# Moving the residual rows and the normalisation between queues and engines in a convolution, Fourier-transform and MLP kernel

## The chip, the core and the metric

The kernel runs on one core of one Trainium2 chip. A core has a matrix engine (TensorE, "PE" in the profile, with "PEld" for the loading of its weights), VectorE ("DVE"), ScalarE ("ACT"), GpSimd ("POOL") and SyncE ("SP"), which computes nothing here and only issues transfers. Each engine works through its own list of instructions in order. Transfers are issued from the lists of SP, ACT and POOL ("SPq", "ACTq", "POOLq" in the profile are the queues of these engines). The metric is the device time in microseconds; the time before is the median of three runs.

## The reference

The input `x` is (8, 4224, 192): eight batches of 4224 rows of 192. Step one is a causal convolution over seven rows with one softmax-weighted filter for each of eight groups of columns. Step two takes its result as the new `x`:

```
X = fft(fft(x, axis=1), axis=2)
u = x + real(X)
un = (u - mean(u)) / sqrt(var(u) + 1e-6)      # over the 192 columns
out = u + relu(un @ w_ch1) @ w_ch2            # 192 -> 768 -> 192
```

All of it is computed for all eight batches in float32, and the big products are made from float16 pairs (a high part and a rest).

## The kernel before

Batches follow each other. For one batch the front part works on whole columns: the convolution as matmuls with a banded matrix (`pc`), whose result `xa` is stored to a scratch tensor `sc` in device memory; loads of `sc` in transform order (`xs`, line 456); their split into a high part `XH` on ScalarE (line 472) and a rest `XL` on VectorE (line 473), both scaled; a first transform stage (`pa`, line 490, copied out as `yh`, `yl`) and a second one (`pb`, line 516, copied out as `V`).

Then come nine tiles for each batch (`it` 0 to 8), the first eight with four groups of 128 rows and the last with one. For a tile, `prep` makes the third transform stage (`pq`, line 574), moves it scaled into `u` (ScalarE, line 591), adds the residual rows `xr` (GpSimd, line 592), takes mean and variance (VectorE, lines 598 and 599), makes the factor `y` and the offset `nm` (lines 610 to 618: the square root on ScalarE, the reciprocal on VectorE, the rest on GpSimd), normalises (`un`, line 628, on ScalarE, apart from the first two tiles of all), and splits into float16 parts `hl` (line 638 on ScalarE, line 641 on GpSimd). A transposing transfer on SP makes `kt` from `hl`. The residual rows are rows of `sc` in an order that four index lists give; `load_res` (line 544) gathers them with one indirect transfer for each group, issued from GpSimd.

The MLP of a tile is `mlp_hidden` (`ph`, line 680; `hh` on ScalarE, line 684; `hlo` on VectorE, line 685) and `mlp_out` (`po`, lines 699, 702 and 705; the sum `u<-po,fo,u` on VectorE, line 711; the store of `u` on SP). `ph` has two buffers in the matrix engine's output memory, and the tag `f` (`pc`, `pa`, `pb`, `pq`) four.

The loop at line 882 gives the order in which all this is written: in step n the MLP's hidden part of tile n, the output part of tile n-1, the normalisation of tile n+2, the transform and sums of tile n+3 and the residual rows of tile n+4 are interleaved with the front part of a later batch. A scheduler then orders every engine's list anew.

Of the kernel before, what the change touches and what calls it, by code (L numbers as in the profile page):

```python
# [125 lines left out]
def kernel(  # L126
# [314 lines left out]
    def load_x(bt, i):  # L441
# [5 lines left out]
        for ch in range(NA // AC):  # L447
# [7 lines left out]
            with tc.issue_after(turn[0]) if b == 1 else ExitStack():  # L455
                load = (nc.scalar if b else nc.sync).dma_start(xs[AC * ch : AC * (ch + 1), : b1 - b0], src)
# [81 lines left out]
    def load_res(bt, it, g):  # L538

        b = bt.b  # L540
        if g == 0:
            bt.xr[it] = sb.tile([128, 4, D], F32, tag="xr", name=f"xr_{b}_{it}", bufs=3)
        col = 0 if it == Q0 else 1 + 4 * it + g
        nc.gpsimd.indirect_dma_start(  # L544
            bt.xr[it][:, g], None, bt.sc[:S],
            bass.IndirectOffsetOnAxis(ap=rows_sb[:, col : col + 1], axis=0),
        )

    def prep(bt, it):
        b = bt.b  # L550
        xr = bt.xr.pop(it)
# [2 lines left out]
        u = sb.tile([128, 4, D], F32, tag="u", name=f"u_{b}_{it}", bufs=5)
# [35 lines left out]
        for to, src in moves:  # L590
            nc.scalar.activation(to, src, AF.Copy, scale=bt.g)  # L591
        nc.gpsimd.tensor_tensor(u[:, :ng], u[:, :ng], xr[:, :ng], op=ALU.add)  # L592
        bt.u[it] = u
# [10 lines left out]
        sd = sb.tile([128, 4], F32, tag="sd", name=f"sd_{b}_{it}", bufs=3)[:, :ng]  # L604
        y = sb.tile([128, 4], F32, tag="y", name=f"y_{b}_{it}", bufs=3)[:, :ng]
        t = sb.tile([128, 4], F32, tag="t", name=f"t_{b}_{it}", bufs=3)[:, :ng]
        w = sb.tile([128, 4], F32, tag="w", name=f"w_{b}_{it}", bufs=3)[:, :ng]
        nm = sb.tile([128, 4], F32, tag="nm", name=f"nm_{b}_{it}", bufs=3)[:, :ng]
        G_ = nc.gpsimd
# [367 lines left out]
```

## Time and profile before

| what | value |
|---|---|
| median of three runs | 1347.4 us (1347.21 to 1353.27) |
| span of the profiled execution | 1331.2 us |
| PE busy | 1198.8 us (90%) |
| ACT busy | 813.4 us (61%) |
| DVE busy | 742.1 us (56%) |
| POOL busy | 660.3 us (50%) |
| mean granted clock of PE | 0.965 |

The span runs from the first to the last instruction of the program on the core. The median lies 16.2 us above it; that is the time around the program. The batches repeat: from about 330 us to 1104 us the same pattern returns every 157 us. Busy time of PE contains modelled ends of pipelined matmuls. A row of a waits view reads "engine line waited for: us in total, times, longest"; a row of a timeline reads "start, length, engine, line, operation, out<-in, count [idle before <- what ended it]"; a row of the groups ends with "busy us, mean ns of one | idle before".

### The profile page before, as it was taken

What the parts mean: (1) busy time and instruction counts of PE and PEld (TensorE: products, weight loads), DVE (VectorE), ACT (ScalarE), POOL (GpSimd) and SP (SyncE); (2) the same over time, 40 slices, a digit from 0 to 9 for tenths busy, and PEclk for the clock granted to TensorE, in tenths of its full rate; (3) what the DMA queues carried; (4) which work ended last, traced back from release to release, by engine and by line L of the source; (5) the groups of instructions that cost most, each with busy time, mean ns of one, the idle gap of its engine ahead of it and who ended that gap; (6) DMA issues with size and microseconds to landing.
All of it is one profiled execution on the core that took longest, in us unless ns stands there. A gap on an engine that the chain in (4) does not pass through costs nothing.

```text
span 1331.2 us, 30081 instructions
## 1 busy us (share of the span) xinstructions
PE 1198.8 (90%) x12224; PEld 942.5 (71%) x12224; DVE 742.1 (56%) x1635; ACT 813.4 (61%) x1562; POOL 660.3 (50%) x1052
## 2 busy tenths in 40 slices
PE   4177889998999989998999989999789998999999
PEld 4175667786878767775877868777577876778667
DVE  7765555466545755456643674446654576555444
ACT  4645766567656775558765676656764667545642
POOL 0255534556345744456435563456634576456520
PEclk9598999998999989999999989999999999999999
DMA  8946855556655555465563566454674443223321
GB/s 270 247 128 152 207 121 122 128 118 158 143 125 118 157 129 135 99 147 147 123 142 103 125 165 142 119 122 114 157 138 109 117 108 84 71 65 81 75 63 40
DMA packets 225819, 170.19 MB, mean 128 GB/s; under 512 B 119560, under 2 KB 207440, under 8 KB 225680
## 3 DMA queue, kind: packets, MB, share of 16 engines
q1 hardware_dynamic: 132048, 85.82, 27.1%
q10 hardware_dynamic: 80960, 56.48, 17.7%
q0 software_dynamic: 12672, 25.97, 7.2%
q8 instruction: 95, 1.56, 0.5%
q14 instruction: 44, 0.36, 0.1%
HBM read 83.73 MB, written 58.55 MB: 107 GB/s over the span
## 4 chain that ended last, share of the span: by engine, by line
POOL 28%; PE 26%; issue 18%; ACT 12%; DMA 8%; DVE 5%; ACTq 1%; POOLq 0%; SPq 0%; DVEq 0%
POOL xr L544 12%; PE ph L680 10%; POOL u L592 6%; DMA sc<-xa 5%; ACT un L628 4%; POOL hl L641 4%; PE po L699 3%; PE po L702 3%; PE po L705 3%; PE pq L574 2%; PE pb L516 2%; ACT hh L684 2%; ACT XH L472 2%; ACT hl L638 2%; DMA xs<-sc 1%
## 5 line engine op out<-in xcount | busy, mean ns | idle before, releaser
L680 PE MATMUL ph<-kt,W 128*128 128x512 f16 (+1 forms) x2160 | 502.3, 366 | 20.3 <-DVE hlo L685 12.4
L685 DVE SCALAR_TENSOR_TENSOR hlo<-ph,hh 128x512 f16<-128x512 f32 (+1 forms) x400 | 271.0, 679 | 405.1 <-ACT hh L684 403.9
L699 PE MATMUL po<-W,hh 128*128 128x192 f16 x1584 | 389.3, 249 | 47.1 <-ACT hh L684 44.3
L702 PE MATMUL po<-W,hh 128*128 128x192 f16 x1584 | 388.8, 249 | 0.0
L705 PE MATMUL po<-W,hlo 128*128 128x192 f16 x1584 | 384.7, 248 | 0.2 <-DVE hlo L685 0.2
L684 ACT ACTIVATE hh<-ph 128x512 f16<-128x512 f32 (+1 forms) x400 | 234.8, 590 | 216.0 <-PE ph L680 147.5
L544 POOL DMA_INDIRECT xr<-sc,rows_sb x264 | 270.5, 1025 | 134.0 <-issue 59.5
L680 PEld LDWEIGHTS <-W 128*128 128x128 f16 x2160 | 195.7, 98 | 169.5 <-issue 32.4
L641 POOL TENSOR_TENSOR hl<-un,hl 128x512 f16<-128x512 f32 (+1 forms) x144 | 126.8, 902 | 187.7 <-ACT hl L638 187.5
L699 PEld LDWEIGHTS <-hh 128*128 128x128 f16 x1584 | 157.1, 99 | 68.0 <-ACT hh L684 49.8
L592 POOL TENSOR_TENSOR u<-u,xr 128x768 f32<-128x768 f32 (+1 forms) x72 | 124.2, 1726 | 154.1 <-ACT u L591 154.0
L628 ACT ACTIVATE un<-u,nm,y 128x192 f32<-128x192 f32 x256 | 120.2, 537 | 98.9 <-POOL nm L618 94.7
L705 PEld LDWEIGHTS <-hlo 128*128 128x128 f16 x1584 | 156.1, 99 | 26.4 <-issue 3.1
L702 PEld LDWEIGHTS <-hh 128*128 128x128 f16 x1584 | 156.7, 99 | 17.6 <-issue 3.3
L387 PE MATMUL pc<-xt,band 128*120 128x144 f32 x756 | 116.4, 292 | 21.4 <-DMA band<-line_d 15.2
L490 PE MATMUL pa<-c_sb,XH 128*128 128x128 f16 x1024 | 104.9, 223 | 24.5 <-ACT XH L472 20.6
L387 PEld LDWEIGHTS pc<-xt,band 128*120 128x120 f32 x756 | 103.0, 186 | 29.0 <-issue 15.2
L473 DVE SCALAR_TENSOR_TENSOR XL<-xs,s_x,XH 128x768 f16<-128x768 f32 x64 | 101.4, 1603 | 20.7 <-ACT XH L472 15.5
L472 ACT ACTIVATE XH<-xs,s_x 128x768 f16<-128x768 f32 x64 | 104.9, 1682 | 9.7 <-DMA xs<-sc 9.7
L490 PEld LDWEIGHTS <-XH 128*128 128x128 f16 x1024 | 83.1, 99 | 36.4 <-ACT XH L472 21.1
L711 DVE SCALAR_TENSOR_TENSOR u<-po,fo,u 128x384 f32<-128x384 f32 (+1 forms) x136 | 81.3, 599 | 40.9 <-PE po L705 39.0
L499 DVE SCALAR_TENSOR_TENSOR yl<-pa,yh 99x512 f16<-99x512 f32 x128 | 85.5, 682 | 30.8 <-ACT yh L498 30.4
(125 smaller groups left out, 1467.2 us busy)
## 6 DMA issues: line engine op xcount, KB each, us to landing
out_dram<-u SPq DMA_DIRECT2D x64, 384.0 KB, 2.4
xt<-in_xw_dram SPq DMA_DIRECT2D x42, 576.0 KB, 7.8
sc<-xa ACTq DMA_DIRECT2D x42, 540.0 KB, 6.1
xs<-sc ACTq DMA_DIRECT2D x84, 192.0 KB, 3.9
xs<-sc ACTq DMA_DIRECT2D x28, 216.0 KB, 3.7
xr<-sc,rows_sb POOLq DMA_INDIRECT x264
sc<-xa ACTq DMA_DIRECT2D x7, 450.0 KB
xt<-in_xv_dram SPq DMA_DIRECT2D x6, 504.0 KB, 4.2
```

The lines of the kernel that those rows point to most:

```text
L387: nc.tensor.matmul(pc[:WR, h - h0], band[:, h, :WR], xt[:, :, h * GRP : (h + 1) * GRP], start=True, stop=True,)
L490: nc.tensor.matmul(pa[:, i], x[:, at], F[:, l], start=(n == 0), stop=(n == 2))
L544: nc.gpsimd.indirect_dma_start(bt.xr[it][:, g], None, bt.sc[:S], bass.IndirectOffsetOnAxis(ap=rows_sb[:, col : col + 1], axis=0),)
L592: nc.gpsimd.tensor_tensor(u[:, :ng], u[:, :ng], xr[:, :ng], op=ALU.add)
L628: nc.scalar.activation(un[:, g], u[:, g], AF.Identity, bias=nm[:, g : g + 1], scale=y[:, g : g + 1],)
L641: nc.gpsimd.tensor_tensor(bl[:, :, o : o + n], un[:, :ng, f], hi[:, :, f], op=ALU.subtract)
L680: nc.tensor.matmul(ph[:, n], W1[:, w, ht * 128 : (ht + 1) * 128], kt[:, k], start=(i == 0), stop=(i == len(order) - 1),)
L684: anchor[0] = nc.scalar.activation(hh, ph, AF.Relu).ins
L685: nc.vector.scalar_tensor_tensor(hlo, ph, 0.0, hh, op0=ALU.max, op1=ALU.subtract)
L699: nc.tensor.matmul(po[:, g % 2], hh[:, ht, tk], W2[:, ht, 0], start=(ht == 0), stop=False)
L702: nc.tensor.matmul(po[:, g % 2], hh[:, ht, tk], W2[:, ht, 1], start=False, stop=False)
L705: nc.tensor.matmul(po[:, g % 2], hlo[:, ht, tk], W2[:, ht, 0], start=False, stop=(ht == 5),)
```

## The change

Five things change together.

Of the four groups of residual rows of a tile, groups 0 and 2 come by two or three strided transfers each, issued from SP; groups 1 and 3, and the one group of the ninth tile, stay indirect transfers from GpSimd. They are written straight into `u`, which takes the place of `xr` and gets eight buffers.

The move of `pq` into `u` and the addition become five VectorE operations (`pq` times `g` plus `u`, written to `u`) in place of three ScalarE moves and one GpSimd addition.

The factor `y` is made on GpSimd alone, from a power of -1/2 and one refinement step; the square root on ScalarE, the reciprocal on VectorE and the offset `nm` go.

`un` and the high part of `hl` are made on GpSimd instead of ScalarE.

The `xs` loads of batches 1 to 7 are issued from SP instead of ScalarE (those of batch 0 already were).

```diff
-                load = (nc.scalar if b else nc.sync).dma_start(xs[AC * ch : AC * (ch + 1), : b1 - b0], src)
+                load = nc.sync.dma_start(xs[AC * ch : AC * (ch + 1), : b1 - b0], src)
...
-            bt.xr[it] = sb.tile([128, 4, D], F32, tag="xr", name=f"xr_{b}_{it}", bufs=3)
-        col = 0 if it == Q0 else 1 + 4 * it + g
-        nc.gpsimd.indirect_dma_start(
-            bt.xr[it][:, g], None, bt.sc[:S],
-            bass.IndirectOffsetOnAxis(ap=rows_sb[:, col : col + 1], axis=0),
-        )
+            bt.u[it] = sb.tile([128, 4, D], F32, tag="u", name=f"u_{b}_{it}", bufs=8)
+        to = bt.u[it][:, g]
+
+        def fetch(part, first, *dims):
+            src = bass.AP(
+                bt.sc.tensor,
+                bt.sc.offset + first * D,
+                [[step * D, n] for step, n in dims] + [[1, D]],
+            )
+            nc.sync.dma_start(part, src)
+
+        if it == Q0 or g % 2:
+            col = 0 if it == Q0 else 1 + 4 * it + g
+            nc.gpsimd.indirect_dma_start(
+                to, None, bt.sc[:S],
+                bass.IndirectOffsetOnAxis(ap=rows_sb[:, col : col + 1], axis=0),
+            )
+            return
+
+        c0 = CG * it
+        cs = -33 if g else 33
+
+        def block(q0, q1, base):
+            fetch(
+                to[CG * (q0 - 1) : CG * (q1 - 1)],
+                base + cs * c0 + 128 * q0, (128, q1 - q0), (cs, CG),
+            )
...
+        if cut > 1:
+            block(1, cut, S)
+        if cut < NQ:
+            block(cut, NQ, 0)
+        if it == 0 and g:
+            fetch(to[0::CG], S // 2 + 128, (128, NQ - 1))
...
-            moves = (
-                (uf[:, 0:4:2], pt[:, :, 0:64]),
-                (uf[:, 1:4:2, :, 0], pt[:, :, 64:0:-1, 0]),
-                (uf[:, 1:4:2, :, 1:3], pt[:, :, 63::-1, 2:0:-1]),
-            )
+            moves = [(uf[:, 2 * t], pt[:, t, 0:64]) for t in range(2)]
+            moves.append((uf[:, 1:4:2, :, 0], pt[:, :, 64:0:-1, 0]))
+            moves += [
+                (uf[:, 2 * t + 1, :, 1:3], pt[:, t, 63::-1, 2:0:-1]) for t in range(2)
+            ]
         for to, src in moves:
-            nc.scalar.activation(to, src, AF.Copy, scale=bt.g)
-        nc.gpsimd.tensor_tensor(u[:, :ng], u[:, :ng], xr[:, :ng], op=ALU.add)
+            nc.vector.scalar_tensor_tensor(
+                to, src, bt.g, to, op0=ALU.mult, op1=ALU.add
+            )
...
-        nc.scalar.activation(sd, var, AF.Sqrt, bias=eps)
-        G_.tensor_scalar(w, var, LNEPS, -0.5, op0=ALU.add, op1=ALU.mult)
-        G_.tensor_scalar(nm, mv[:, :ng, 0], -1.0, None, op0=ALU.mult)
-        nc.vector.reciprocal(y, sd)
-        G_.tensor_tensor(t, y, y, op=ALU.mult)
-        G_.tensor_tensor(t, t, w, op=ALU.mult)
-        G_.tensor_scalar(t, t, 1.5, None, op0=ALU.add)
-        G_.tensor_tensor(y, y, t, op=ALU.mult)
-        G_.tensor_tensor(nm, nm, y, op=ALU.mult)
+        P.tensor_scalar(v, var, LNEPS, None, op0=ALU.add)
+        P.tensor_tensor(y, v, minus_half[:, :ng], op=ALU.pow)
+        P.tensor_tensor(t, y, y, op=ALU.mult)
+        P.tensor_tensor(t, t, v, op=ALU.mult)
+        P.tensor_scalar(t, t, -0.5, 1.5, op0=ALU.mult, op1=ALU.add)
+        P.tensor_tensor(y, y, t, op=ALU.mult)
...
-                nc.scalar.activation(
-                    un[:, g], u[:, g], AF.Identity,
-                    bias=nm[:, g : g + 1], scale=y[:, g : g + 1],
-                )
+            nc.gpsimd.tensor_scalar(
+                un[:, g], u[:, g], mv[:, g, 0:1], y[:, g : g + 1],
+                op0=ALU.subtract, op1=ALU.mult,
+            )
...
-        nc.scalar.activation(hi, un[:, :ng], AF.Copy)
+        nc.gpsimd.tensor_copy(hi, un[:, :ng])
```

The scheduler's order moves with it. Three places matter below; all lie where tile 1 of batch 3 is in the MLP and the `xs` of batch 4 are split. In a name such as `hh_3_1_8326` the first two numbers are batch and tile, the last a running number.

ScalarE, before:

```order
L684 ACTIVATE hh_3_1_8326<-ph_3_1_2_8461 128x512
L472 ACTIVATE XH_106<-xs_4_2_8273,s_x4_7887 128x64x12 x2
L456 DMA xs_4_3_8398<-sc_4_6175 32x8x192
L628 ACTIVATE un_3_3_8336<-u_3_3_8226,nm_3_3_8313,y_3_3_8310 128x192 x4
L456 DMA xs_4_3_8398<-sc_4_6175 32x8x192 x3
L684 ACTIVATE hh_3_1_8326<-ph_3_1_3_8499 128x512
L343 ACTIVATE sq_5_0_8509,nrm_5_8508<-xt_5_0_8109 128x1152
L638 ACTIVATE hl_3_3_8392<-un_3_3_8336 128x4x192
L684 ACTIVATE hh_3_1_8326<-ph_3_1_4_8547 128x512
```

and with the change:

```order
L708 ACTIVATE hh_3_1_8195<-ph_3_1_2_8330 128x512
L708 ACTIVATE hh_3_1_8195<-ph_3_1_3_8369 128x512
L345 ACTIVATE sq_5_0_8379,nrm_5_8378<-xt_5_0_7982 128x1152
L474 ACTIVATE XH_106<-xs_4_2_8146,s_x4_7764 128x64x12 x2
L708 ACTIVATE hh_3_1_8195<-ph_3_1_4_8417 128x512
L708 ACTIVATE hh_3_1_8195<-ph_3_1_5_8440 128x512
L708 ACTIVATE hh_3_2_8450<-ph_3_2_0_8452 128x512
L474 ACTIVATE XH_106<-xs_4_3_8267,s_x4_7764 128x64x12 x2
```

Nothing that GpSimd makes and no `xs` load stands between the `hh` any more.

VectorE, before:

```order
L685 SCALAR_TENSOR_TENSOR hlo_3_1_8327<-ph_3_1_2_8461,hh_3_1_8326 128x512
L473 SCALAR_TENSOR_TENSOR XL_107<-xs_4_2_8273,s_x4_7887,XH_106 128x64x12 x2
L711 SCALAR_TENSOR_TENSOR u_3_0_7463<-po_3_0_2_8477,fo_393,u_3_0_7463 128x384
L685 SCALAR_TENSOR_TENSOR hlo_3_1_8327<-ph_3_1_3_8499,hh_3_1_8326 128x512
L685 SCALAR_TENSOR_TENSOR hlo_3_1_8327<-ph_3_1_4_8547,hh_3_1_8326 128x512
L685 SCALAR_TENSOR_TENSOR hlo_3_1_8327<-ph_3_1_5_8575,hh_3_1_8326 128x512
L598 BN_STATS st_3_5_8738<-u_3_5_8638 128x6 x4
```

and with the change:

```order
L709 SCALAR_TENSOR_TENSOR hlo_3_1_8196<-ph_3_1_3_8369,hh_3_1_8195 128x512
L475 SCALAR_TENSOR_TENSOR XL_107<-xs_4_2_8146,s_x4_7764,XH_106 128x64x12
L625 SCALAR_TENSOR_TENSOR u_3_5_8265<-pq_3_5_8502,g_3_5474,u_3_5_8265 128x192 x2
L625 SCALAR_TENSOR_TENSOR u_3_5_8265<-pq_3_5_8502,g_3_5474,u_3_5_8265 128x2x64
L625 SCALAR_TENSOR_TENSOR u_3_5_8265<-pq_3_5_8502,g_3_5474,u_3_5_8265 128x64x2 x2
L475 SCALAR_TENSOR_TENSOR XL_107<-xs_4_2_8146,s_x4_7764,XH_106 128x64x12
L709 SCALAR_TENSOR_TENSOR hlo_3_1_8196<-ph_3_1_4_8417,hh_3_1_8195 128x512
L632 BN_STATS st_3_5_8603<-u_3_5_8265 128x6 x4
```

The five additions for tile 5 stand between the two halves of an `XL` piece, ahead of `hlo` 4.

SP, before (`xt` are the convolution's inputs of batch 5):

```order
L651 DMA_TRANSPOSE kt_3_2_8262<-hl_3_2_8179 128x12x128
L330 DMA xt_5_1_8324<-in_xw_dram 128x1152
L719 DMA out_1_dram<-u_3_0_7463 128x768
L651 DMA_TRANSPOSE kt_3_3_8456<-hl_3_3_8392 128x12x128
L330 DMA xt_5_2_8583<-in_xw_dram 128x1152
```

and with the change:

```order
L553 DMA u_3_6_8490<-sc_3_3791 128x1x192
L553 DMA u_3_6_8490<-sc_3_3791 112x1x192
L553 DMA u_3_6_8490<-sc_3_3791 16x1x192
L553 DMA u_3_7_8777<-sc_3_3791 128x1x192 x2
L675 DMA_TRANSPOSE kt_3_2_8135<-hl_3_2_8052 128x12x128
L332 DMA xt_5_1_8193<-in_xw_dram 128x1152
L458 DMA xs_4_2_8146<-sc_4_6084 32x8x192 x4
L458 DMA xs_4_3_8267<-sc_4_6084 32x8x192 x4
L743 DMA out_1_dram<-u_3_0_7058 128x768
L675 DMA_TRANSPOSE kt_3_3_8325<-hl_3_3_8261 128x12x128
```

The second half of the `xs` loads now stands on SP behind a transposition and an `xt` load, and the residual rows of tile 6 stand ahead of the transposition of tile 2.

More of the change, by code (lines that the diff above doesn't have):

```diff
@@ L151 @@
     nc.vector.memset(ones, 1.0)
-    eps = cp.tile([128, 1], F32, name="eps")
-    nc.vector.memset(eps, LNEPS)
-    nc.scalar.activation(cp.tile([128, 1], F32, name="warm"), eps, AF.Sqrt)
+    minus_half = cp.tile([128, 4], F32, name="minus_half")
+    nc.vector.memset(minus_half, -0.5)
+    nc.scalar.activation(
+        cp.tile([128, 1], F32, name="warm"), ones[:, 0:1], AF.Sqrt
+    )
     def exp_nonpositive(x):
@@ L273, in load @@
         def load(rows, n, name):
-            t = sb.tile([128, HID], F32, tag="u", name=name, bufs=5)
+            t = sb.tile([128, HID], F32, tag="u", name=name, bufs=8)
             from_float64(t[:rows, :n], raws[name][:, :n], rows, n, name)
@@ L541, in load_res @@
         if g == 0:
[L542 to L547 removed]
+            bt.u[it] = sb.tile([128, 4, D], F32, tag="u", name=f"u_{b}_{it}", bufs=8)
[21 more added lines that the diff above has]
+            )
+        cut = 1
+        while 128 * cut + min(cs * c0, cs * (c0 + CG - 1)) < 0:
+            cut += 1
+        if cut in (2, NQ - 1):
+            cut += 1
+        if cut > 1:
[4 more added lines that the diff above has]
+            fetch(to[0::CG], S // 2 + 128, (128, NQ - 1))
     def prep(bt, it):
         b = bt.b
[L551 removed]
         ng = 1 if it == Q0 else 4
         pq = ps.tile([128, ND, 2, NC], F32, tag="f", name=f"pq_{b}_{it}", bufs=4)
[L554 removed]
+        u = bt.u[it]
         if it == Q0:
@@ L584, in prep @@
         else:
-            moves = (
-                (uf[:, 0:4:2], pt[:, :, 0:64]),
-                (uf[:, 1:4:2, :, 0], pt[:, :, 64:0:-1, 0]),
-                (uf[:, 1:4:2, :, 1:3], pt[:, :, 63::-1, 2:0:-1]),
-            )
[L590 to L593, printed above, removed]
+            moves = [(uf[:, 2 * t], pt[:, t, 0:64]) for t in range(2)]
[3 more added lines that the diff above has]
+            ]
+        for to, src in moves:
+            nc.vector.scalar_tensor_tensor(
+                to, src, bt.g, to, op0=ALU.mult, op1=ALU.add
+            )
         yield
@@ L603, in prep @@
         var = mv[:, :ng, 1]
[L604 to L609, printed above, removed]
-        nc.scalar.activation(sd, var, AF.Sqrt, bias=eps)
-        G_.tensor_scalar(w, var, LNEPS, -0.5, op0=ALU.add, op1=ALU.mult)
-        G_.tensor_scalar(nm, mv[:, :ng, 0], -1.0, None, op0=ALU.mult)
-        nc.vector.reciprocal(y, sd)
-        G_.tensor_tensor(t, y, y, op=ALU.mult)
-        G_.tensor_tensor(t, t, w, op=ALU.mult)
-        G_.tensor_scalar(t, t, 1.5, None, op0=ALU.add)
-        G_.tensor_tensor(y, y, t, op=ALU.mult)
-        G_.tensor_tensor(nm, nm, y, op=ALU.mult)
+        v, t, y = (
+            sb.tile([128, 4], F32, tag=n, name=f"{n}_{b}_{it}", bufs=3)[:, :ng]
+            for n in ("v", "t", "y")
+        )
+        P = nc.gpsimd
+        P.tensor_scalar(v, var, LNEPS, None, op0=ALU.add)
[4 more added lines that the diff above has]
+        P.tensor_tensor(y, y, t, op=ALU.mult)
         yield
```

6 lines of the change are left out of this document (1 added, 5 removed).

## The prediction

> **What bounds the kernel now.** I read the page's busy times first, then who waited for whom, then windows over one batch, then the timeline of the worst window.
>
> ```profile
> span 1331.2 us, 30081 instructions
> PE 1198.8 (90%) x12224; PEld 942.5 (71%) x12224; DVE 742.1 (56%) x1635; ACT 813.4 (61%) x1562; POOL 660.3 (50%) x1052
> PE po L699 <- ACT hh L684: 44.3, 26, 4.6
> PE pa L490 <- ACT XH L472: 20.6, 2, 16.8
> PE ph L680 <- DVE hlo L685: 12.4, 23, 1.4
> PE ph L680 <- DMA kt<-hl: 7.2, 1, 7.2
> PE pa L490 <- DVE XL L473: 2.2, 3, 0.9
> ```
>
> PE is busy for 1198.8 of 1331.2 us, so an engine that gets lighter pays only through the 132 us in which PE stands still. Of these 44.3 us are `po` waiting for ScalarE's `hh`; the change touches this wait. The 20.6 us for `XH` lie at the start (16.8 in one piece), ahead of everything the change moves.
>
> ```profile
> 609.10:640.80 31.70, 25.88 (x210) 19.00 (x208) 21.99 (x38) 24.89 (x38) 21.97 (x29) 0.89 0.63 168
> 628.33:637.30 8.97, 8.97 (x56) 6.17 (x57) 4.25 (x13) 7.93 (x15) 5.05 (x6) 0.73 0.67 153
> 640.80:766.20 125.40, 122.39 (x1325) 97.89 (x1323) 63.93 (x152) 76.81 (x161) 60.46 (x104) 1.00 0.54 124
> ```
>
> The columns after start, end and length are busy time (and instructions) of PE, PEld, DVE, ACT and POOL, then PE's clock. A batch repeats every 157.1 us and falls into a **dense zone** of 31.7 us, from the first `XL` of the next batch to the last, in which PE is busy for 25.88, and the rest, in which PE is busy for 122.39 of 125.4. So at most 3 us for each batch lie outside the zone. In the zone 5.8 us are idle, and 2.4 more go to the clock, which is 0.73 over 8.97 us (0.27 x 8.97).
>
> ```profile
> 625.94 0.55 ACT L628 ACTIVATE un<-u,nm,y 128x192 f32<-128x192 f32 x1 [2.83 <-POOL nm L618]
> 627.70 0.57 ACT L684 ACTIVATE hh<-ph 128x512 f16<-128x512 f32 x1
> 628.33 0.34 PE L699 MATMUL po<-W,hh 128*128 128x192 f16 x1 [4.47 <-ACT hh L684]
> 620.87 1.17 POOL L544 DMA_INDIRECT xr<-sc,rows_sb  x1 [0.30 <-issue]
> 622.07 1.34 POOL L615 TENSOR_TENSOR t<-t,w 128x4 f32<-128x4 f32 x1
> 623.49 1.35 POOL L611 TENSOR_SCALAR w<-mv 128x4 f32<-128x4 f32 x1
> 621.84 2.99 DVE L473 SCALAR_TENSOR_TENSOR XL<-xs,s_x,XH 128x768 f16<-128x768 f32 x2
> 626.13 0.20 POOL L615 TENSOR_TENSOR t<-t,w 128x4 f32<-128x4 f32 x1
> ACT un L628 <- POOL nm L618: 94.7, 58, 3.9
> ```
>
> This is how the zone's hole of 4.47 us comes about. GpSimd gathers rows, its small operations take 1.34 us beside VectorE's `XL` instead of 0.20, `nm` is late, ScalarE stands at `un`, and `hh` stands behind `un`. Over the run ScalarE waits 94.7 us in this place.
>
> **ScalarE.** What leaves it, for a tile of four groups:
>
> ```profile
> L591 ACT ACTIVATE u<-pq,g 128x384 f32<-128x384 f32 x64 | 37.5, 586 | 9.9 <-PE pq L574 6.4 <-DVE hlo L685 2.0 <-DMA out_dram<-u 1.5
> L591 ACT ACTIVATE u<-pq,g 128x256 f32<-128x256 f32 x64 | 31.1, 486 | 0.0
> L591 ACT ACTIVATE u<-pq,g 128x128 f32<-128x128 f32 x64 | 28.3, 442 | 0.0
> L628 ACT ACTIVATE un<-u,nm,y 128x192 f32<-128x192 f32 x256 | 120.2, 537 | 98.9 <-POOL nm L618 94.7 <-DMA sc<-xa 3.8 <-POOL hl L641 0.3
> L638 ACT ACTIVATE hl<-un 128x768 f16<-128x768 f32 x64 | 53.5, 836 | 4.8 <-issue 3.2 <-DVE un L623 1.5
> L456 ACTq DMA_DIRECT2D xs<-sc x112: 309/461/1840, 98.0 to 1103.1; - x112
> ACT hh L684 <- DMA sc<-xa: 45.6, 10, 5.5
> ```
>
> 1.51 us of moves, four `un` of 0.54 and 0.84 of `hl` make 4.5 us for a tile, 288 us over 64 tiles; ScalarE falls from 813 to about 520. The 112 loads (0.46 us each) leave its queue, and with them most of the 45.6 us in which `hh` stood behind a wait for the stores of `xa`. I take all of the 4.47 us hole and its clock loss as removed at this place, bounded by nothing (another engine steps in) and 6.9 us.
>
> **VectorE.** It gets five operations for a tile.
>
> ```profile
> L711 DVE SCALAR_TENSOR_TENSOR u<-po,fo,u 128x384 f32<-128x384 f32 x128 | 78.0, 610 | 39.2 <-PE po L705 38.1
> L711 DVE SCALAR_TENSOR_TENSOR u<-po,fo,u 128x192 f32<-128x192 f32 x8 | 3.3, 417 | 1.7 <-PE po L705 0.9 <-DMA out_dram<-u 0.2
> L473 DVE SCALAR_TENSOR_TENSOR XL<-xs,s_x,XH 128x768 f16<-128x768 f32 x56 | 86.2, 1560 | 18.0 <-ACT XH L472 12.8 <-DMA xs<-sc 5.2
> ```
>
> L711 has the same form (matmul output times a factor plus `u`): 0.42 us for 192, 0.61 for 384, so 1.0 ns an element and 0.35 us for 128. Two of 192 and three of 128 make 1.89 us; the bounds are 1.51 (ScalarE's three moves) and 3.05 (five at 0.61). Over 64 tiles that is 121 us, and VectorE goes to about 850. In the dense zone of before it worked 21.99 us; one tile's additions fall between the first and the last `XL`, which makes 23.6. PE's work there at full clock is 25.88 - 2.4 = 23.5. The two are level, and the end of the zone has no room:
>
> ```profile
> 639.16 1.55 DVE L473 SCALAR_TENSOR_TENSOR XL<-xs,s_x,XH 128x768 f16<-128x768 f32 x1
> 641.10 0.22 PE L490 MATMUL pa<-c_sb,XL 128*128 128x128 f16 x1
> ```
>
> The last `XL` ends at 640.71, and its first reader starts at 641.10. So **VectorE's `XL` is late next**, 0.4 us behind the wait removed. The zone will last between 23.6 (both engines full) and 31.7 (as now). I take 27.5, VectorE 86% busy, nearer the rest of the batch, where PE reaches 98%, than the zone as it is. That saves 4.2 us of 31.7.
>
> **GpSimd.** It loses 128 gathers and the additions and gets `un` and the high part.
>
> ```profile
> L544 POOL DMA_INDIRECT xr<-sc,rows_sb x264 | 270.5, 1025 | 134.0 <-issue 59.5 <-DMA xt<-in_xw_dram 56.1 <-POOL u L592 14.5
> L592 POOL TENSOR_TENSOR u<-u,xr 128x768 f32<-128x768 f32 x64 | 119.5, 1868 | 140.8 <-ACT u L591 140.7
> L592 POOL TENSOR_TENSOR u<-u,xr 128x192 f32<-128x192 f32 x8 | 4.7, 590 | 13.3 <-ACT u L591 13.3
> L531 POOL COPY V<-V 128x96 f16<-128x96 f16 x64 | 16.9, 266 | 98.6 <-DVE V L525 97.8
> L616 POOL TENSOR_SCALAR t<-t 128x4 f32<-128x4 f32 x64 | 14.5, 227 | 4.8
> ```
>
> Gone: 128 x 1.025 = 131, and 124 of additions. The small operations are seven before and six after; apart from the power they are a draw, at 0.23 each. `un` lies between 0.27 (the copy of 96) and 0.59 (an addition of 192): I take 0.43, 264 x 0.43 = 114. The high part lies between 0.27 and 1.87: I take 1.0, 64 us. The power has no row: at least 0.2 like its neighbours, and nothing bounds it from above; I take 0.5, 36 us. GpSimd comes to 660 - 131 - 124 + 114 + 64 + 36 = 619. That is hidden: only `kt` waits for it, and PE waited for `kt` once in the run (the 7.2 us, at the start).
>
> The Trainium skill says in "GPSIMD Engine Reference", section "Engine selection", that elementwise work belongs on VectorE and GpSimd is about half as fast with two inputs, though near line rate with one. By that, `un` would be at the lower end of its range and the sum stays.
>
> **SP.** 192 strided transfers and 112 loads come, 304 x 0.46 = 140 us of issuing.
>
> ```profile
> SPq L719 <- DVE u L711: 471.3, 50, 14.1
> 95.86 0.20 POOL L611 TENSOR_SCALAR w<-mv 128x4 f32<-128x4 f32 x1
> 86.72 0.17 DVE L599 BATCH_NORM_AGGREGATE mv<-st 128x2 f32<-128x6 f32 x1
> ```
>
> SP stands for 471 us at one store alone, so there is time. A load that waits for a free `xs` buffer now holds up what follows it: stores of `u`, transpositions, rows of later tiles. By the order, the rows are issued two to three tiles ahead. I price the queue at +2 us, between 0 and the rival below.
>
> **The start.** `mv` is ready at 86.9, but `w` starts at 95.86 behind eight gathers, and the first `ph` waits 7.2 us for `kt`. With the change all early gathers stand ahead of the first normalisation. I take 7 of the 7.2. About 3 us of the 44.3 also lie in the first batch.
>
> **The sum.** Six zones at 4.2: 25. Outside them, 1.3 of at most 3 us for each of six batches: 8. Start 7 + 3, last batch 1, SP -2. That is 42 us, so the span is 1289. The median lies 16.2 above the span, so **1305 us**.
>
> **The rivals.** *PE alone decides (faster).* VectorE hides its additions in idle time: each zone gives 6.9 us, the rest 2.5, the start 10: 6 x 9.4 + 10 = 66 us, 1281. For it: VectorE idles 9.7 us in the zone now. Against it: the 0.4 us at the zone's end.
>
> *SP's queue takes the place of ScalarE's wait.* The second half of the `xs` loads stands behind a transposition, which waits for GpSimd, and an `xt` load. If they come 4 us later, `XH` and `XL` follow, the zone gives nothing, and 42 - 25 leaves 17 us: 1330. Against it: SP's idle time.
>
> *GpSimd and VectorE get in each other's way (slower).* The small operations' 1.34 us show that one of the two waits. Now GpSimd reads SBUF for `un` and the high part where it gathered. If each of the eight `XL` of a zone waits for one high part, 1.4 us (between the 1.0 taken above and the bound of 1.87), the zone goes from 27.5 to 38.7, 7 us longer than now: 42 - 17 = 25 us more, 1372. It decides from 0.9 us an `XL` up, where the zone is 34.5 and its loss of 6 x 2.8 eats the other 17 us. Against it: `XL` averages 1.56 us now, beside GpSimd's additions.
>
> The Trainium skill states this as a rule in "SBUF — State Buffer", section "Who interferes with whom": a VectorE operation with two SBUF inputs and a GpSimd operation that reads SBUF exclude each other, and the later one waits in full. The stretched rows agree for GpSimd as the loser; no row here shows VectorE as the loser.
>
> *The power is slow (slower).* A batch takes about 150 us, and GpSimd's other work is (619 - 36) / 8 = 73, so nine powers decide from 8.6 us each. At 11 GpSimd needs 172 a batch, 15 more than now: 8 x 15 = 120, about 1467.
>
> **How the numbers follow.** Chances: forecast (1290 to 1318) 0.46, PE alone 0.18, SP 0.18, interference 0.12, slow power 0.06. A run tells no change from within 0.5%, that is 1340.7 to 1354.1. Faster: 0.46 + 0.18 + 0.14 of SP = 0.78; same: 0.04 of SP and 0.01 of interference; slower: the remaining 0.17. The low end is PE alone with a little more, 1268; the high end takes in SP's rival and the beginning of interference, 1352.
>
> **What would show it.** Right: no wait of ScalarE for GpSimd; `po` on `hh` under 10 us in all; the clock near 1 in the zone; `pa` on `XL` or `ph` on `hlo` as the largest PE wait after the start; VectorE near 850 and GpSimd near 620 busy; additions of 0.42 and 0.35 us. Wrong: `XH` or `XL` waiting for the `xs` transfers; `XL` well over 1.56 us; a power of many us; PE waiting for `kt`.

## The result and the profile after

The changed kernel takes **1309.94 us** (median of four runs, 1306.4 to 1311.85) against 1347.31 us for the kernel before in the same group of runs: a ratio of **0.9715**, 95% interval 0.9689 to 0.9741. In a second group it took 1306.94 us against 1345.65, a ratio of 0.9722 (0.9700 to 0.9744). The forecast was 1305.

One reading of the part before the prediction has to be corrected first. The changed kernel's profiled run took 1310.74 us and its span is 1308.4, so only 2.3 us lie around the span, not 16.2. The kernel before was therefore run twice more for its trace: 1328.39 us with a span of 1326.6 in one group of runs, 1349.43 us with a span of 1347.6 in another. The profile of before that the prediction read, with its span of 1331.2, belongs to the first kind, and the median of 1347.4 to the second. The 16.2 us are then, by these two runs, the difference between groups of runs. So ratios are always taken inside one group here, and spans of the changed kernel are compared with the span of 1347.6.

From the page of the changed kernel the busy times, then its waits of PE (us in total, times, longest us):

```profile
PE 1191.7 (91%) x12224; PEld 938.2 (72%) x12224; DVE 828.9 (63%) x1883; ACT 585.2 (45%) x962; POOL 794.4 (61%) x1116
...
PE ph L704 <- DVE hlo L709: 17.1, 8, 2.9
PE po L723 <- ACT hh L708: 16.7, 6, 4.3
PE pa L492 <- issue: 11.2, 12, 2.6
```

ScalarE has got lighter by 228 us, VectorE heavier by 87, GpSimd heavier by 134 instead of lighter. `po` waits 16.7 us for `hh` instead of 44.3, and ScalarE never waits for GpSimd at `un` any more, since no `un` is left on it. The wait for `kt` at the start is nearly gone (0.8 us). New against the recorded profile are 11.2 us of `issue` at `pa`; `issue` is idle time for which the profile shows nothing that the engine waited for.

One batch, in windows (start, end, length; busy of PE, PEld, DVE, ACT, POOL; PE's clock, DMA share, GB/s):

```profile
606.20:635.20 29.00, 23.64 (x179) 16.34 (x178) 23.02 (x41) 17.87 (x20) 21.67 (x25) 0.88 0.79 178
635.20:760.40 125.20, 124.59 (x1357) 100.49 (x1356) 74.61 (x182) 55.66 (x102) 76.56 (x116) 1.00 0.50 125
626.00:632.00 6.00, 4.46 (x15) 2.25 (x16) 4.10 (x12) 2.10 (x3) 4.43 (x7) 0.50 0.53 159
```

The dense zone (first to last `XL`) has shrunk from 31.7 to 29.0 us, and outside it PE is now full: 124.59 of 125.20 us. All that is left to gain in a batch lies in the zone, where 5.4 us are idle and the clock is half for six more, a loss of 3 us. The timeline there shows what the idle time is (start, length, engine, line, operation, tiles, and in brackets the idle time before it with what ended it):

```profile
606.35 1.47 SPq L675 DMA_TRANSPOSE kt<-hl  x1
607.86 0.89 SPq L332 DMA_DIRECT2D xt<-in_xw_dram  x1
609.45 1.88 DVE L475 SCALAR_TENSOR_TENSOR XL<-xs,s_x,XH 128x960 f16<-128x960 f32 x1
611.36 4.56 SPq L458 DMA_DIRECT2D xs<-sc  x4
...
620.82 3.11 ACT L474 ACTIVATE XH<-xs,s_x 128x768 f16<-128x768 f32 x2 [2.62 <-DMA xs<-sc]
623.84 1.05 ACT L708 ACTIVATE hh<-ph 128x512 f16<-128x512 f32 x2
624.47 0.26 PE L723 MATMUL po<-W,hh 128*128 128x192 f16 x1 [2.79 <-ACT hh L708]
...
622.46 1.53 DVE L475 SCALAR_TENSOR_TENSOR XL<-xs,s_x,XH 128x768 f16<-128x768 f32 x1 [3.69 <-ACT XH L474]
623.91 1.55 DVE L625 SCALAR_TENSOR_TENSOR u<-pq,g,u 128x192 f32<-128x192 f32 x5
625.37 1.52 DVE L475 SCALAR_TENSOR_TENSOR XL<-xs,s_x,XH 128x768 f16<-128x768 f32 x1
626.80 0.68 DVE L709 SCALAR_TENSOR_TENSOR hlo<-ph,hh 128x512 f16<-128x512 f32 x1
627.54 1.03 PE L704 MATMUL ph<-kt,W 128*128 128x512 f16 x2 [2.57 <-DVE hlo L709]
```

The row of the kernel before for the same four loads, issued from ScalarE:

```profile
613.58 1.81 ACTq L456 DMA_DIRECT2D xs<-sc  x4
```

Two holes stand where one of 4.47 us stood. The third piece's `xs` loads stand on SP after a transposition and an `xt` load. SP is through with both at 608.75, but the loads need a free buffer: the first goes out at 611.36, when the first piece's last `XL` ends (609.45 and 1.88 us). The four issues then take 4.56 us instead of 1.81. ScalarE stands 2.62 us for them at `XH`; `hh` is behind `XH`, and PE waits 2.79 us. Then VectorE has two `XL` and a tile's five additions to do one after the other, `hlo` is behind them, and PE waits 2.57 us more. The middle five of the seven zones show the same pair (2.8 to 4.3 us and 2.3 to 2.6 us).

What the moved operations cost (groups; busy us, mean ns of one):

```profile
L652 POOL TENSOR_SCALAR un<-u,mv,y 128x192 f32<-128x192 f32 x264 | 279.0, 1063 | 7.9 <-POOL y L648 0.2
L644 POOL TENSOR_TENSOR y<-v,minus_half 128x4 f32<-128x4 f32 x64 | 75.5, 1180 | 3.2
L625 DVE SCALAR_TENSOR_TENSOR u<-pq,g,u 128x192 f32<-128x192 f32 x136 | 50.6, 410 | 10.0 <-PE pq L608 10.0
L475 DVE SCALAR_TENSOR_TENSOR XL<-xs,s_x,XH 128x768 f16<-128x768 f32 x56 | 87.6, 1580 | 40.9 <-ACT XH L474 40.8
```

VectorE's additions cost what was said (0.36 and 0.41 us), and so does the high part (0.95 us a tile for 1.0). `un` costs 1.06 us instead of 0.43, outside the bounds of 0.27 and 0.59.

### The profile page after: what moved, and what is told of

The parts are those of the page before. It is cut to its first block, busy times and chain, and to the rows that moved or that the text cites. A ratio compares the mean times of both kernels' runs of the same rounds, so it can differ in the third digit from the quotient of the medians.

```text
span 1308.4 us, 30213 instructions
## 1 busy us (share of the span) xinstructions
PE 1191.7 (91%) x12224; PEld 938.2 (72%) x12224; DVE 828.9 (63%) x1883; ACT 585.2 (45%) x962; POOL 794.4 (61%) x1116
## 3 DMA queue, kind: packets, MB, share of 16 engines
q8 instruction: 95, 1.56, 0.5%
## 4 chain that ended last, share of the span: by engine, by line
PE 74%; DMA 9%; DVE 8%; ACT 3%; issue 2%; another core or an unknown queue 1%; ACTq 1%; POOL 1%; SPq 1%; DVEq 0%; POOLq 0%
PE ph L704 28%; PE po L723 8%; PE po L729 8%; PE po L726 8%; DMA xs<-sc 6%; PE pa L492 6%; PE pc L389 5%; PE pb L518 5%; PE pq L608 5%; DVE XL L475 3%; DVE u L625 2%; ACT XH L474 2%; DMA sc<-xa 1%; DVE hlo L709 1%
## 5 line engine op out<-in xcount | busy, mean ns | idle before, releaser
L704 PE MATMUL ph<-kt,W 128*128 128x512 f16 (+1 forms) x2160 | 504.9, 367 | 22.3 <-DVE hlo L709 17.1
L723 PE MATMUL po<-W,hh 128*128 128x192 f16 x1584 | 387.8, 247 | 16.9 <-ACT hh L708 16.7
L652 POOL TENSOR_SCALAR un<-u,mv,y 128x192 f32<-128x192 f32 x264 | 279.0, 1063 | 7.9 <-POOL y L648 0.2
L557 POOL DMA_INDIRECT u<-sc,rows_sb x136 | 144.6, 1063 | 195.5 <-DMA xt<-in_xw_dram 56.4
L665 POOL TENSOR_TENSOR hl<-un,hl 128x512 f16<-128x512 f32 (+1 forms) x144 | 122.2, 870 | 2.8
L500 ACT ACTIVATE yh<-pa 99x512 f16<-99x512 f32 x128 | 75.5, 598 | 87.3 <-PE pa L492 63.6
L643 POOL TENSOR_SCALAR v<-mv 128x4 f32<-128x4 f32 (+1 forms) x72 | 20.7, 287 | 152.9 <-DVE mv L633 150.2
```

The costliest lines, as they stand in the source:

```text
L557: nc.gpsimd.indirect_dma_start(to, None, bt.sc[:S], bass.IndirectOffsetOnAxis(ap=rows_sb[:, col : col + 1], axis=0),)
L652: nc.gpsimd.tensor_scalar(un[:, g], u[:, g], mv[:, g, 0:1], y[:, g : g + 1], op0=ALU.subtract, op1=ALU.mult,)
L704: nc.tensor.matmul(ph[:, n], W1[:, w, ht * 128 : (ht + 1) * 128], kt[:, k], start=(i == 0), stop=(i == len(order) - 1),)
L723: nc.tensor.matmul(po[:, g % 2], hh[:, ht, tk], W2[:, ht, 0], start=(ht == 0), stop=False)
```

## The experiments

Twelve runs were made, in three groups of four, each group on another chip. The kernel before measured 1332.3, 1345.65 and 1347.94 us in them, so a comparison of two variants across groups is weaker than one inside a group. A scheduler orders every engine's list anew for each variant. PE's order moves little with three buffers on the changed kernel, with the `xt` loads on ScalarE and with the `xs` loads undone (in the traces some 170 to 190 lines differ among 12,224 matmuls), and more where the rows, the additions or the normalisation are undone (1300 to 1800), so those differences hold a new order as well.

| kernel | time, us | before in its group, us | ratio to before | 95% interval |
|---|---|---|---|---|
| changed kernel | 1309.94 | 1347.31 | 0.9715 | 0.9689 to 0.9741 |
| the same, second group | 1306.94 | 1345.65 | 0.9722 | 0.9700 to 0.9744 |
| normalisation undone | 1301.35 | 1332.3 | 0.9780 | 0.9749 to 0.9810 |
| rows and additions undone | 1368.16 | 1332.3 | 1.0281 | 1.0245 to 1.0317 |
| xs loads undone | 1282.47 | 1332.3 | 0.9640 | 0.9605 to 0.9675 |
| rows and additions alone | 1318.65 | 1345.65 | 0.9795 | 0.9760 to 0.9830 |
| additions undone | 1291.68 | 1347.94 | 0.9590 | 0.9551 to 0.9629 |
| xt loads from ScalarE | 1312.80 | 1347.94 | 0.9761 | 0.9710 to 0.9813 |
| **three xs buffers** | **1285.17** | 1345.65 | **0.9553** | 0.9530 to 0.9576 |
| three xs buffers, xs loads undone | 1302.61 | 1345.65 | 0.9694 | 0.9662 to 0.9725 |
| three xs buffers, normalisation undone | 1312.62 | 1347.94 | 0.9734 | 0.9695 to 0.9773 |

### The kernel before, twice, and the changed kernel again

No edit.

> The kernel before, once more, for its span beside its own time. The changed kernel's time lay 2.3 us above its span (1310.74 and 1308.4), while the prediction took 16.2 us for what lies around the span. If the kernel before really has 16 us around its span, this gives a span of about 1331 and a time of about 1347. If the profiled execution of before was only a short one, time and span lie about 2.3 us apart here too.

> The kernel before, a second time for its trace. Its times fell into two groups so far, 1328 to 1336 us in one group of runs and 1340 to 1353 in two others, and each profile of a variant in the latter two has 14 us in which PE, ScalarE and VectorE stand for 'issue' between 65 and 85 us. Theory: that stretch belongs to the chip, not to the change; where this run takes 1340 us or more, it has it, too, and where it takes about 1330, it has not. Rival: the strided rows cause it; then it is never there.

> The changed kernel once more, beside the others of this group. In its first profile all engines but GpSimd and SP stood for some 14 us between 67 and 83 us, waiting for 'issue', which neither the kernel before nor any variant shows. If that belongs to this program, the ratio to the kernel before stays at 0.9715 or worse and the stretch is there again. If it was an accident of that execution or that chip, the stretch is gone, the span falls to about 1294 us, and the start gains the 10 us that the prediction gave it.

The kernel before took 1328.39 us with a span of 1326.6, and 1349.43 us with 1347.6: about 2 us lie around the span each time. The start, in windows of 10 us (PE's busy time is the first after the length), of the changed kernel, of the kernel before in its longer run, and of the variant with the additions undone, which ran in the same group as the latter:

```profile
65.00:75.00 10.00, 4.16 (x43) 3.00 (x40) 1.41 (x3) 2.69 (x6) 7.58 (x8) 0.84 0.66 174
75.00:85.00 10.00, 4.41 (x35) 3.71 (x36) 3.17 (x6) 3.74 (x7) 2.84 (x3) 0.50 0.20 57
```

```profile
65.00:75.00 10.00, 6.05 (x73) 5.56 (x72) 3.36 (x5) 4.80 (x9) 6.71 (x8) 0.84 0.28 78
75.00:85.00 10.00, 8.69 (x99) 8.16 (x98) 7.15 (x11) 6.25 (x11) 0.00 (x0) 0.68 0.01 2
```

```profile
65.00:75.00 10.00, 8.33 (x119) 7.83 (x118) 5.88 (x9) 8.82 (x17) 4.30 (x5) 0.82 0.32 105
75.00:85.00 10.00, 9.02 (x153) 8.35 (x151) 7.51 (x13) 6.94 (x14) 0.53 (x2) 1.00 0.01 3
```

In the changed kernel PE works only 8.6 of the 20 us between 65 and 85, and waits for `issue` at `pa` (11.2 us); its repetition has the same stretch (9.15 of 20). The kernel before has a shorter one (14.7 of 20) in this run and none in the recorded profile; in the group where the kernel before took 1332 us no variant has it, with or without strided rows. So neither theory holds as written: the stretch comes with the group of runs (each on its own chip), and it is longer where the rows of many tiles are fetched at the start. With the additions undone the rows go into three buffers instead of eight, and there is none. What the engines' sequencers wait for is not in the trace; this stays open.

### Normalisation undone, and rows and additions alone

```diff
-        P.tensor_tensor(y, v, minus_half[:, :ng], op=ALU.pow)
+        nc.scalar.activation(sd, var, AF.Sqrt, bias=eps)
...
-            nc.gpsimd.tensor_scalar(
-                un[:, g], u[:, g], mv[:, g, 0:1], y[:, g : g + 1],
-                op0=ALU.subtract, op1=ALU.mult,
-            )
+                nc.scalar.activation(
+                    un[:, g], u[:, g], AF.Identity,
+                    bias=nm[:, g : g + 1], scale=y[:, g : g + 1],
+                )
...
-        nc.gpsimd.tensor_copy(hi, un[:, :ng])
+        nc.scalar.activation(hi, un[:, :ng], AF.Copy)
```

The shortened edit above is that of the first kernel. The second is the kernel before with the change's rows and additions alone.

> The changed kernel with the normalisation as before: square root, un and the high part on ScalarE, the reciprocal on VectorE (rows, additions and loads stay changed). The prediction's account (the hole of a zone is ScalarE standing at un for GpSimd's nm): the hole comes back, 4 us for each of six zones and the 1.3 us outside them, so 1335 to 1345 us. Rival: the gathers ahead of the small operations were the cause, and half of them stay away: then ScalarE waits little, the time stays within 1305 to 1318, and since GpSimd's un of 1.06 us goes, the start gains up to 7 us.

> The kernel before with the rows alone changed (strided transfers on SP for half of them, VectorE's additions in u); normalisation on ScalarE and xs loads from ScalarE as before. The prediction's account (the hole is ScalarE standing at un for GpSimd): it stays, about 4 us for each zone; VectorE's additions come on top: ratio 0.985 to 1.00. Rival (the gathers and additions on GpSimd made nm late, and they are gone): the hole goes without moving the normalisation, ratio 0.965 to 0.975.

Undoing the normalisation alone gives 0.9780. That is the upper end of the rival's range (1318 of 1347) and far from the 0.991 or more of the prediction's account. With the `xs` loads undone as well it is 0.9795, between the two expectations. The waits of the first:

```profile
PE po L731 <- ACT hh L716: 31.2, 12, 5.0
ACT un L660 <- POOL nm L650: 27.9, 26, 2.9
ACT XH L472 <- DMA xs<-sc: 21.1, 6, 7.2
```

ScalarE's wait for `nm` falls from 94.7 us (64.8 in the run of before with the span of 1347.6) to 27.9, and 25.6 with the rows alone, although `un` is back on ScalarE. So taking half the gathers and the additions off GpSimd removes some two thirds of that wait, and moving `un` the rest. In the dense zones, where it made the hole (2.7 to 3.9 us in each of the last six), it is gone altogether with the rows and additions alone. But PE's wait for `hh` does not go. It stays at 31.2 us with the normalisation undone, where in four of the middle five zones ScalarE stands 2.2 to 2.8 us at `XH` just before the hole, in three of them for the late `xs` loads. It stays at 23.7 us with the rows alone, where ScalarE's list stands at `xs` loads that it issues itself. Rows and additions alone are worth 2%.

### Rows and additions undone, and additions alone undone

The first puts back four gathers into `xr`, ScalarE's moves and GpSimd's addition; the second fetches the rows as the changed kernel does, but into `xr` with three buffers, and puts back the moves and the addition:

```diff
-            nc.vector.scalar_tensor_tensor(
-                to, src, bt.g, to, op0=ALU.mult, op1=ALU.add
-            )
+            nc.scalar.activation(to, src, AF.Copy, scale=bt.g)
+        nc.gpsimd.tensor_tensor(u[:, :ng], u[:, :ng], xr[:, :ng], op=ALU.add)
```

> The changed kernel with the residual rows as before: four gathers on GpSimd into a buffer of their own, moves on ScalarE, addition on GpSimd (normalisation and loads stay changed). The prediction's account: GpSimd gets 131 us of gathers and 124 of additions on top of 794, some 1050 us, 130 of the 154 us of a batch, so kt comes later but not late; ScalarE's queue holds the moves; 1315 to 1330 us. Rival (VectorE's additions set the end of the zone, the second hole of 2.6 us before ph): without them that hole goes, 6 x 2.6 us, and the time falls to about 1295.

> The changed kernel with the additions as before (rows fetched half by strided transfers, but into a buffer of their own; moves on ScalarE, addition on GpSimd). With rows and additions both undone GpSimd was busy for 1033 us, kt came 8 to 12 us late once a batch and the ratio was 1.028. If the additions' 124 us on GpSimd decide that, the ratio stays at 1.00 to 1.02 (GpSimd about 900 us). If the gathers' 131 us in the queue decide it, the waits for kt go and the ratio is 0.97 to 0.98.

1.0281 and 0.9590, both outside what was expected: their edits differ in nothing but the 128 gathers, and they lie 7% apart, far more than the groups of runs do. With rows and additions undone (busy times; the wait of PE):

```profile
PE 1196.6 (88%) x12224; PEld 937.5 (69%) x12224; DVE 749.2 (55%) x1555; ACT 662.1 (49%) x1162; POOL 1033.0 (76%) x1316
PE ph L672 <- DMA kt<-hl: 78.5, 9, 17.3
```

With the additions alone undone:

```profile
PE 1187.7 (92%) x12224; PEld 938.5 (73%) x12224; DVE 750.9 (58%) x1555; ACT 660.7 (51%) x1162; POOL 904.5 (70%) x1188
PE ph L705 <- DMA kt<-hl: 8.8, 4, 7.0
598.59 1.82 SPq L458 DMA_DIRECT2D xs<-sc  x4
592.79:619.53 26.74, 24.25 (x219) 18.25 (x216) 21.96 (x36) 20.93 (x29) 23.14 (x24) 1.00 0.82 191
```

With 1033 us of work GpSimd is late for `kt` by 5.5 to 12.5 us once a batch; with 904 it is not. So half the gathers had to go for the normalisation to fit on GpSimd, and the change with normalisation and loads alone would have been slower than before. The second variant also beats the changed kernel (0.9590 to 0.9722, in different groups): its zone is 26.7 us at full clock in three batches (in two others 29.6 and 31.9, with a hole of 2.6 us before `po`), VectorE has 1.1 us less to do in it (21.96 for 23.02), and the four `xs` issues take 1.82 us; in this order they go out ahead of the transposition. How much of the 1.3% belongs to VectorE and how much to the issues these runs don't separate.

### xs loads undone

```diff
-                load = nc.sync.dma_start(xs[AC * ch : AC * (ch + 1), : b1 - b0], src)
+                load = (nc.scalar if b else nc.sync).dma_start(xs[AC * ch : AC * (ch + 1), : b1 - b0], src)
```

> The changed kernel with the xs loads issued from ScalarE again (all else stays changed). The prediction's account prices SP's queue at 2 us: 1306 to 1314 us. Rival (SP's queue is the new wait: in a zone XH stands 2.6 us for loads whose four issues take 4.5 us instead of 1.8, and hh and po stand behind it): the first hole of each zone, 2.8 to 4.3 us, goes, and the time falls to 1285 to 1295 us.

0.9640 (0.9605 to 0.9675), below the changed kernel's interval, but measured in the other group of runs, where the changed kernel did not run. Its wait of PE for `hh`, and its zone:

```profile
PE po L723 <- ACT hh L708: 14.6, 7, 2.8
583.63:611.89 28.26, 23.15 (x200) 16.87 (x197) 24.18 (x41) 18.78 (x21) 25.11 (x27) 1.00 0.77 183
```

The hole before `po` is still there (2.2 to 2.8 us), and the other one too (1.5 to 1.7). The third piece's loads start when the buffer is free, as late as in the changed kernel (5.2 us after the zone begins), and go out in 1.82 us; but the fourth piece's now take 4.3 us to issue from ScalarE, and `hh` stands behind them there. PE works 1.6 us between the two holes (0.5 in the changed kernel), and in four zones of five the clock stays at 1.00. PE idles 5.1 us in this zone, hardly less than the changed kernel's 5.4; the batch is 3 us shorter (150.5 for some 153.5), as much as the halved clock had cost. That moving the loads cost something is likely from the ratios, but not settled across groups; moving them back does not take the hole away, so the rival's 1285 to 1295 us rested on a wait that only changed its place. (The 1282 us are a time of the group in which the kernel before took 1332.)

### xt loads from ScalarE

```diff
-            nc.sync.dma_start(xt, src[:, ch * WC : (ch + 1) * WC])
+            (nc.scalar if b > 1 else nc.sync).dma_start(xt, src[:, ch * WC : (ch + 1) * WC])
```

> The changed kernel with the transform-input loads xt of the third batch and later issued from ScalarE. In a zone xt (0.9 us) and a transposition go out from SP ahead of the third piece's loads, whose four issues then take 4.5 us, 1.8 where ScalarE issues them. Queue theory: with xt off SP the issues take about 1.8 us, the first hole shrinks by 2.7 us in each of five zones, 13 us: ratio 0.960 to 0.964. Buffer theory (the loads start too late, whatever their speed): ratio 0.970 to 0.974.

0.9761, no better than the changed kernel. Without `xt` ahead of them the issues take as long (4.9 us for the four at 607.83), they start at the same moment, and the hole is larger:

```profile
PE po L723 <- ACT hh L708: 28.8, 7, 6.0
ACT XH L474 <- DMA xs<-sc: 46.4, 9, 7.7
```

The `xt` load in SP's queue is not the cause.

### Three xs buffers

```diff
-        tag, bufs = (("yh", 1), ("yl", 1))[i - 2] if b == 0 and i > 1 else ("xs", 2)
+        tag, bufs = (("yh", 1), ("yl", 1))[i - 2] if b == 0 and i > 1 else ("xs", 3)
```

(and the same number in the four other places that use the tag)

> The changed kernel with three xs buffers instead of two: the third piece's loads need not wait for the first piece to be split. SP theory (XH stands for loads that start only when a buffer is free and whose issues take 4.5 us): the first hole of each zone, 2.8 to 4.3 us, goes, some 18 us, a ratio of about 0.958. Rival (the 16 transfer engines are the limit there, busy 0.97 over the hole): the same bytes take the same time, the hole only moves; ratio as the changed kernel's. Prediction's account (VectorE sets the end of the zone): the second hole of 2.3 to 2.9 us stays and grows a little; a gain of 5 us at most.

> The changed kernel with xs loads from ScalarE and three xs buffers. With the loads from ScalarE the ratio was 0.964, and two holes of 1.6 and 2.8 us were left in each zone. If loads that are late are still the cause of one of them, the third buffer takes it: 6 x 2.8 us, ratio about 0.952. If the two remedies take the same wait: 0.964. If VectorE sets these holes: 0.962 to 0.966.

> The fastest so far (three xs buffers, ratio 0.955) with the normalisation back on ScalarE. The prediction's account (ScalarE stands at un for nm, beside XL, whatever the loads do): the hole of about 4 us in each zone comes back, ratio 0.972 to 0.978. Rival (with half the gathers gone and the loads early, ScalarE has the time): 0.953 to 0.960.

The third buffer on the changed kernel gives **0.9553**, 22 us less than the changed kernel in the same group and 60 less than the kernel before. The theory of late loads had said about 0.958. SP's list, in which the batch number is left out of the names, shows what it moved: the third piece's loads (`xs_2`) go out some 40 us earlier, ahead of another tile's transposition, instead of behind a transposition and an `xt` load:

```
 L458 DMA xs_1_3544<-sc_1482 32x8x192 x2
+L458 DMA xs_2_3560<-sc_1482 32x8x192 x2
 L675 DMA_TRANSPOSE kt_0_3042<-hl_0_2985 128x12x128
...
 L675 DMA_TRANSPOSE kt_2_3549<-hl_2_3466 128x12x128
 L332 DMA xt_1_3607<-in_xw_dram 128x1152
-L458 DMA xs_2_3560<-sc_1482 32x8x192 x4
```

The zone and the rest of one batch, three rows of VectorE in the zone, and PE's wait for `hh` over the run:

```profile
593.53:616.91 23.38, 21.82 (x190) 16.09 (x188) 22.57 (x41) 18.33 (x21) 20.45 (x20) 1.00 0.73 187
616.91:740.30 123.39, 122.93 (x1340) 99.07 (x1338) 73.70 (x180) 54.19 (x100) 79.81 (x120) 1.00 0.55 133
604.28 3.04 DVE L475 SCALAR_TENSOR_TENSOR XL<-xs,s_x,XH 128x768 f16<-128x768 f32 x2
607.75 0.70 DVE L709 SCALAR_TENSOR_TENSOR hlo<-ph,hh 128x512 f16<-128x512 f32 x1
609.27 1.23 DVE L625 SCALAR_TENSOR_TENSOR u<-pq,g,u 128x192 f32<-128x192 f32 x4
PE po L723 <- ACT hh L708: 1.1, 2, 0.8
```

In this batch both holes are gone, as in three others, and over the run `po` waits 1.1 us for `hh`. The second hole went with the first: with the loads in time `hlo` stands between the two `XL` and the additions and no longer behind both, although VectorE's work in the zone is about the same (22.57 us). The zone is 23.4 us long and the clock stays at 1.00. A batch takes 146.8 us, of which PE works 144.7, and the gain lies in the batches: 876.0 us from the last `XL` of the second to that of the eighth, for 901.3 in the changed kernel's run of the same group. Two later zones still have holes before `ph` of 1.3 to 2.0 us. So neither the transfer engines (the rival) nor VectorE's load as such set the zone of the changed kernel, but loads that go out late and slowly. The traces tell two parts apart. The buffer sets the start: in each of the five zones the first load goes out within 0.04 us of the end of the first piece's last `XL`, also with the loads on ScalarE and with `xt` off SP. The queue sets the pace: on SP the four issues then take 3.8 to 5.6 us, issued some 40 us earlier they take 1.9. Three buffers take away both, so what each costs alone was not measured.

With the loads on ScalarE the third buffer gives 0.9694, which none of the three expectations named: the remedy doesn't work there, and a batch takes 150.4 us as with two buffers. With the normalisation back on ScalarE it gives 0.9734, in the range of the prediction's account. ScalarE waits for `nm` again, but not at the hole (ScalarE, then PE in the same zone):

```profile
ACT un L660 <- POOL nm L650: 19.8, 29, 1.8
620.92 1.86 ACT L660 ACTIVATE un<-u,nm,y 128x192 f32<-128x192 f32 x4
622.68 0.59 ACT L716 ACTIVATE hh<-ph 128x512 f16<-128x512 f32 x1
623.16 3.15 ACT L472 ACTIVATE XH<-xs,s_x 128x768 f16<-128x768 f32 x2
626.19 0.84 ACT L670 ACTIVATE hl<-un 128x768 f16<-128x768 f32 x1
626.92 0.59 ACT L716 ACTIVATE hh<-ph 128x512 f16<-128x512 f32 x1
627.57 0.26 PE L731 MATMUL po<-W,hh 128*128 128x192 f16 x1 [2.00 <-ACT hh L716]
```

The normalisation's move is worth 1.8% here, some 24 us, compared across two groups. But the account of the hole is another than the prediction's. ScalarE has no idle time in the 9 us before the hole of 2.0 us, and of the 19.8 us only 1.1 lie in the five zones. `un` and `hl`, 2.7 us a tile, stand in its list among `XH` and `hh`: it is ScalarE's work that makes `hh` late, no longer its wait for GpSimd. Three buffers together with the additions undone were not tried.

## Why the prediction was right, and where it was not

**The time** was 1305 and is 1307 to 1310. The sum it came from was 42 us; measured inside one group it is 37 and 39. But its parts are not all right, and that they came out so close is in part luck, as the batches show.

**What lay around the span.** "The median lies 16.2 above the span" was no part of the kernel. It did no harm, since 42 us were taken from a median, and only the base was named wrongly.

**ScalarE, the hole, and the wait for `nm`**: the hole of before was read rightly, and with all parts together the wait is gone. That moving `un` is what removes it is not what the runs show: in the zones the wait is gone as soon as half the gathers and the additions are off GpSimd. What moving `un` and `hl` brings there is room in ScalarE's list. ScalarE is busy for 585 us, not 520: all its instructions together fell from 935 to 621 us, by 314, but 121 us of those before overlapped one another, so adding up durations of single rows overstates what the busy time loses.

**VectorE**: right in size, 829 for 850, and 23.02 us in the zone for 23.6 (the terms shown, 21.99 and 1.89, make 23.9). "`XL` is late next" was nearly right: in the recorded run `hlo` behind two `XL` and the additions is the larger of the two holes' sums (17.1 against 16.7 us).

**The zone** was to be 27.5 us and is 29.0 and, a batch later, 28.7. PE and VectorE work there as forecast; the step that failed is "the queue at +2 us". It took SP's idle time as enough and each issue at 0.46 us; the four issues of the third piece take 4.56 us, and the 192 strided transfers 0.70 us each at the median. (Groups 0 and 2 of 64 tiles are 128 groups, so they come by one to three transfers each.) The loads of the third piece cost the hole of 2.8 to 4.3 us, `po` on `hh` stays at 16.7 us where under 10 were expected, and the clock, which was to be near 1, is 0.88. That the second hole follows from the first, and that both go with a third buffer, was seen neither in the forecast nor in the rival for SP's queue. That rival had the right place ("behind a transposition") and the right chain (`XH`, then `XL`), but not the reason: the loads don't wait for the transposition, whose issue is over 3.5 us before they start; they wait for the buffer and are then issued slowly. It priced the zone at no gain; 22 us is what the late loads are worth in the run with three buffers.

**GpSimd** was to be busy for 619 us and is for 794. `un` was taken at 0.43 us and takes 1.06: 165 us too little. The power was taken at 0.5 and takes 1.18 with four columns: 44 too little. The other small operations were called a draw, seven before against six with the power; without it they are five, and take 92 us for 126: 34 too much. "That is hidden" holds, but with little room: with the 128 gathers and the additions on top `kt` is late by some 9 us a batch. At 619 us the prediction thought the gathers a mere relief; they are what makes the rest possible.

The Trainium skill's "GPSIMD Engine Reference", section "Engine selection", was cited for one-input work near line rate. The conversion agrees (0.95 us for 768 elements, 1.2 ns each), `un` does not (1.06 us for 192, 5.5 ns each); the measurement decides.

**The batches and the start.** From the last `XL` of the second batch to that of the eighth the recorded profile of before takes 930.5 us, the changed kernel 905.7 and 901.3: 25 to 29 us for the 33 of the sum (zones 25, outside them 8). Against the run of before with the span of 1347.6 (938.8) it is 33 to 37. That this meets the 33 is luck: the six zones gave 16 to 18 us of it instead of 25, and the time between them 15 to 21 instead of 8. The start was to give 10: `kt` is no longer waited for (0.8 us for 7.2), but 2.6 to 4.5 us is all that is gained up to the last `XL` of the second batch against the run of before with the span of 1347.6, and the stretch of `issue` is longer than there by 6 us of PE's idle time (8.6 and 14.7 busy of 20). The end after the eighth batch's `XL` gives 3, not 1.

**The rivals.** *PE alone decides* is what three buffers reach: 1285 us, where 1281 was worked out. *Interference* fell: `XL` takes 1.58 us (1.56 before). It is GpSimd that waits, as the prediction's rows showed: three `un` next to two `XL` take 5.24 us instead of 3.

```profile
921.18 3.03 DVE L475 SCALAR_TENSOR_TENSOR XL<-xs,s_x,XH 128x768 f16<-128x768 f32 x2
920.72 5.24 POOL L652 TENSOR_SCALAR un<-u,mv,y 128x192 f32<-128x192 f32 x3
```

By the Trainium skill's rule ("SBUF — State Buffer", section "Who interferes with whom") the later of the two waits; the trace agrees where GpSimd is the later one: the `un` that starts at 921.71, after the first `XL`, takes 3.25 us. It shows no loss where VectorE is: that `XL` starts at 921.18 while an `un` runs (920.72 to 921.72) and takes 1.56 us as elsewhere. There the measurement decides. *The slow power* fell: 1.18 us, not 8.6.

## What to carry to other kernels

A part that is booked as hidden should be tried against the true load of the engine that hides it: here half the gathers looked like spare room and were what kept GpSimd in time. When work moves to another queue, look at what stands ahead of it there and whether its buffer is free in time; one more buffer, which lets the loads go out early, took away two holes that looked like two engines' limits. A hole can come back in the same place for another reason, so look each time at what the engine did just before it. And a profile and a median may come from different groups of runs, so compare a span with the time of its own run.
